# Pooled q and k in four buffers, v of batch 0 pooled by additions, mask cast on GpSimd, and a new order from the planner

## The chip, the cores and the metric

The kernel runs on one core of a Trainium2 chip. The core has a matrix engine (TensorE, PE in the profile; PEld is its weight load), three engines for elementwise work (VectorE, DVE; ScalarE, ACT; GpSimd, POOL) and a queue engine (SyncE, SP) that issues most of the transfers from device memory. Each engine works through a list of its own in order; they meet at semaphores. The metric is the time of one execution on the device in microseconds.

## What is computed

Attention over 4 batches of 8 heads with 576 positions of 64 channels, in two parts that are added: one on q, k and v averaged over groups of four positions (144 each), whose result is repeated four times, and one in a band of 7 keys around each position. Its output, 2304 rows of 512 channels, goes through two feed-forward blocks. All in float32.

```python
q_d, k_d, v_d = (x.reshape(B, H, S // 4, 4, D).mean(axis=3) for x in (q, k, v))
out_up = np.repeat(sm_attn(q_d, k_d, v_d), 4, axis=2)
mask = np.abs(pos[:, None] - pos[None, :]) < 4
out_local = softmax(where(mask, scale * q @ k.T, -1e9)) @ v
x = (out_up + out_local).transpose(0, 2, 1, 3).reshape(2304, 512)
...
h = x @ w_in                     # 512 -> 2048
x = (s * np.maximum(h, 0) ** 2 + b) @ w_out
...
out = ((x @ w_a) * (x @ w_b)) @ w_out2   # 512 -> 1536 -> 512
```

## The kernel before

The matmuls of the feed-forward blocks run at full TensorE speed on numbers split in a high and a low part (`xsh`, `xsl`; `gh`, `gl`), with three products for each. The weights come as 64-bit words; a slice of 512 KB (`w_a`, `w_o`) is turned into its two parts on ScalarE and VectorE in steps (ScalarE's L349, L342 and L378, VectorE's L354, L362 and L383). The first block has 32 slices. It works on six blocks of 384 positions with 16 steps each: a step has 12 products `h` (L1059 to L1061), then ScalarE's relu (L1076), square (L1080) and cast (L1083), then VectorE's rest `gl` (L1087), then 12 products `acc` (L1102 to L1104). The second block (`ab`, L1347) comes behind.

Attention has to deliver a block's x before its first `h`. Two stages do it. In the ramp stand the first eight band tiles of 96 positions, the pooled part of batches 0 and 1, and all 32 weight slices. In the band stage, which opens only behind the last task of the ramp, because it takes over its memory, the remaining positions are worked on VectorE (L908, L914, L969), along with the pooled parts of batches 2 and 3.

The pooled part goes by pairs of heads, four for a batch. For a pair: load k and q, sum groups of four into `kd`, `qd` (VectorE L582 for batch 0, GpSimd L584 and L585 for batch 1), scores `sc` on TensorE (L620), maximum `nb` (L634), its scaling (L637), exponentials on ScalarE (L647), a normalizing product (L662), transposes `at` (L671), copies (L683), then the product with pooled v, `o` (L691), copied to `up` (L703). For batch 0 the pooled v, `vp`, is a reduction on VectorE (L603). For the other batches `pv` is summed by transfers: SyncE issues a plain one (L549) for each half of the keys, and GpSimd issues three that accumulate onto each (L551), six in all. A band tile has scores (L774, L780), exponentials (L816), transposes (L839) and `o` (L857).

What stands where in each engine's list is decided by a planner in the kernel's own Python. Every piece of work is a task with an engine, an estimated duration, what it reads, the buffers and tokens that it takes and gives back, and a due time. `Program.order` always takes the task that can start earliest, and of equal ones the one due first; it also puts filler products `pw` on `wz` between TensorE's ramp tasks. Instructions are emitted in that order. Buffer counts (`RAMP_BUFS`) and tokens limit how far a list can run ahead: loaded slices have four tokens, `MAX_STAGED`. Durations and due times are constants in the source, so a change of them changes the order of the lists and nothing else.

Of the kernel before, what the change touches and what calls it, by code (L numbers as in the profile page):

```python
# [23 lines left out]
TQ = 96  # L24
# [31 lines left out]
MAX_STAGED = 4  # L56

# [3 lines left out]
T0, STEP = 40.2, 4.018 / 384  # L61
LEAD = 26.6
DUE_DOWN = (12.1, 7.8, 2.1, 22.5)
DUE_NEXT = (60.0, 0.0)
DUE_TILE = (8.3, 20.6, 22.0)
DUE_JOB = (11.6, 11.7, 14.9)

WARM, FILL_MIN, FILL_MAX = 18, 1, 20

RAMP_BUFS = {"dq": 2, "dk": 2, "dv": 2, "qd": 1, "kd": 1, "vp": 4, "tq": 1, "tk": 1, "tv": 2, "e": 1, "x": 1, "z": 2}  # L70
# [39 lines left out]
class Program:  # L110
# [26 lines left out]
    def order(self):  # L137
# [9 lines left out]
        clock, warming = Clock(), True  # L147
# [10 lines left out]
        while len(out) < len(self.tasks):  # L158
            best = None
            for e in ENGINES:  # L160
                for t in avail[e]:
                    s = max(at[e], t.ready)
                    picks, fs = [], []
# [42 lines left out]
            at[t.eng] = t.end  # L206
            avail[t.eng].remove(t)
# [26 lines left out]
def moe_chain(ctx, tc, qT, kT, vd, tq, tk, tv, qu, ku, vu, w_a1, w_o1, w_a2, w_b2, w_o2, sb, ident_d, bmask_d, emask_d, out):  # L234
# [19 lines left out]
    ones = const.tile([128, 2], F32, name="ones")  # L254
    bc = const.tile([128, HP], F32, name="bc")
# [19 lines left out]
    def load(dst_src, nbytes, reads=(), writes=(), acq=(), rel=(), due=1e9, after=()):  # L275
# [18 lines left out]
    def i_fn(picks):  # L294
        nc.sync.dma_start(out=ident, in_=ident_d)
        V.tensor_copy(out=identb, in_=ident[:TQ, :TQ])

    def m_fn(picks):
        bm = new("r", "tq", [128, HP, TQ])[:TQ].rearrange("p a b -> p (a b)")[:, :3 * TW].rearrange("p (a b) -> p a b", a=3)
        nc.sync.dma_start(out=bm, in_=bmask_d)  # L300
        V.tensor_copy(out=bmaskb, in_=bm)
# [3 lines left out]
    def consts():  # L305
        add("SP", 0.5, i_fn, writes=["ident"])
        add("SP", 0.5, m_fn, writes=["const"], acq=[("rtq",)], rel=["rtq"])
# [99 lines left out]
    def w_out(p, t, after, due=1e9):  # L407
# [8 lines left out]
        if t == 0:  # L416
# [12 lines left out]
            wait = [add("SP", 1.5, s_fn, [("wz", t, p)], [("wod", p)])]  # L429
# [109 lines left out]
    def pool_in(b, after, due):  # L539
# [18 lines left out]
    def down(b, hp, ph, pool_eng, v_eng, due=1e9):  # L558
# [16 lines left out]
        for name, src in (("k", "dk"), ("q", "dq")):  # L575
            eng = pool_eng[name == "q"]

            def prep(p, name=name, eng=eng):
# [9 lines left out]
                eng, dve(S) if eng == "DVE" else 1.25, prep, [(src, key)], [(name + "d", key)],  # L588
                [(ph + name + "d",)], [ph + (dq if src == "dq" else src)] if b else (),
            )  # L590
        if b == 0:
            for kh in range(2):
                def lv(p, kh=kh):
                    st["v", kh] = new(ph, "dv", [HK, 4, 2 * D])
                    return st["v", kh], vd[b, hp, :, kh]

                load(lv, HK * 2048, writes=[("dv", key, kh)], acq=[(ph + "dv",)], after=after)

                def vprep(p, kh=kh):
                    x = st["v", kh]  # L600
                    d = st["vp", kh] = new(ph, "vp", [HK, 2 * D])
                    if v_eng == "DVE":
                        V.tensor_reduce(out=d, in_=x.rearrange("p r c -> p c r"), axis=AX.X, op=ALU.add)  # L603
                    else:
                        G.tensor_tensor(out=x[:, 0:2], in0=x[:, 0:2], in1=x[:, 2:4], op=ALU.add)
                        G.tensor_tensor(out=d, in0=x[:, 0], in1=x[:, 1], op=ALU.add)

                add(
                    v_eng, dve(512) if v_eng == "DVE" else 1.1, vprep, [("dv", key, kh)], [("vp", key, kh)],
                    [(ph + "vp",)], [ph + "dv"],  # L610
                )

        def vpool(kh):
            return st["vp", kh] if b == 0 else pooled[b][:, kh, hp]

        def s_fn(p):
# [9 lines left out]
            "PE", 1.0, s_fn, [("qd", key), ("kd", key)], [("sc", key)], [wide, wide, E_SLOT[ph]],  # L626
# [49 lines left out]
        tt = add("PE", 0.55, t_fn, [("a", key), "ident"], [("at", key)], [wide, wide], lead=LEAD, share=0.5625)  # L676
# [10 lines left out]
        def o_fn(p):  # L687
# [9 lines left out]
            "PE", 0.6, o_fn, [("aT", key), ("upslot", b)] + ([("vp", key, 0), ("vp", key, 1)] if b == 0 else [("pv", b)]),  # L697
            [("o", key)], [wide], [pick(ts, 2)] + ([ph + "vp", ph + "vp"] if b == 0 else ["pv"] if hp == HP - 1 else []),
# [845 lines left out]
    for hp in range(HP):  # L1544
        down(0, hp, "r", DOWN_ENG[hp], "DVE", target(0) - DUE_DOWN[0] + DUE_DOWN[1] * hp)
# [145 lines left out]
```

## Time and profile before

| | |
|---|---|
| median of 3 runs | 935.74 us (934.76 to 935.96) |
| span of the profiled execution, first to last instruction | 932.3 us |
| TensorE busy | 913.2 us, 98% |
| VectorE busy | 789.9 us, 85% |
| ScalarE busy | 497.4 us, 53% |
| GpSimd busy | 69.7 us, 7% |
| moved by transfers | 96.76 MB, 104 GB/s in the mean |

The profile is of one execution; its page gives the span, not the whole time of that execution, which holds 3.4 us more if it was like the median. Busy shares are means over stages that differ: a row of a window tells more than the page's first line. Busy time of TensorE includes the filler products.

### The profile page before, as it was taken

How to read it: one execution, taken by the hardware profiler on the slowest of the kernel's cores; microseconds unless marked ns; L12 is line 12 of the kernel's file. 1: busy time of each engine (PE TensorE's matmuls, PEld its weight loads, DVE VectorE, ACT ScalarE, POOL GpSimd, SP SyncE). 2: the span in 40 equal slices, each digit the busy share in tenths (PEclk: the TensorE clock that was granted, in tenths of full speed). 3: DMA queues.
4: the chain of work that ended last, by engine and by line, in shares of the span. 5: the costliest groups of instructions: out<-in, count | busy, mean ns of one | idle time of the engine just before them, and what ended most of it. 6: DMA issues, size and time to landing. Idle time of an engine off the chain costs nothing.

```text
span 932.3 us, 14367 instructions
## 1 busy us (share of the span) xinstructions
PE 913.2 (98%) x5319; PEld 847.0 (91%) x5319; DVE 789.9 (85%) x1388; ACT 497.4 (53%) x1144; POOL 69.7 (7%) x70
## 2 busy tenths in 40 slices
PE   8988999999999999999999999999999999999997
PEld 4667989998999899999999999999999999999996
DVE  6988998999999999995977999879877778877753
ACT  4989995345445443535988555335433336433322
POOL 2241201021322200000000000000000000000000
PEclk9998999999999999999999999999999999999999
DMA  7869626224354332313477342012200010300001
GB/s 206 241 174 332 156 90 194 82 82 133 115 115 114 103 107 69 102 29 136 148 262 261 122 122 82 23 44 81 102 22 3 24 43 13 102 29 18 1 1 69
DMA packets 46864, 96.76 MB, mean 104 GB/s; under 512 B 6393, under 2 KB 21337, under 8 KB 46409
## 3 DMA queue, kind: packets, MB, share of 16 engines
q1 hardware_dynamic: 39160, 92.77, 31.0%
q0 software_dynamic: 7200, 2.67, 2.5%
q8 instruction: 42, 0.69, 0.3%
q10 hardware_dynamic: 432, 0.39, 0.1%
q14 instruction: 30, 0.24, 0.1%
HBM read 83.22 MB, written 12.58 MB: 103 GB/s over the span
## 4 chain that ended last, share of the span: by engine, by line
PE 84%; DVE 5%; ACT 4%; issue 3%; DMA 2%; POOL 1%; SPq 0%; ACTq 0%
PE ab L1347 28%; PE acc L1102 7%; PE acc L1103 6%; PE h L1059 6%; PE acc L1104 6%; PE h L1061 6%; PE h L1060 6%; PE acc L1488 5%; PE acc L1489 5%; PE acc L1487 5%; DVE pr L969 1%; DMA pv<-in_vd_dram 1%; ACT z L342 1%; DMA tq<-in_bmask_dram 1%; ACT w L378 1%
## 5 line engine op out<-in xcount | busy, mean ns | idle before, releaser
L1347 PE MATMUL ab<-xo,w 128*128 128x384 f32 x1376 | 273.7, 338 | 0.4 <-DVE u L1390 0.4
L1347 PEld LDWEIGHTS ab<-xo,w 128*128 128x128 f32 x1376 | 246.1, 188 | 16.3 <-DVE u L1390 0.7
L1102 PE MATMUL acc<-gh,w 128*128 128x384 f32 (+1 forms) x384 | 134.2, 350 | 4.0 <-ACT w L816 2.0
L1103 PE MATMUL acc<-gl,w 128*128 128x384 f32 x384 | 131.2, 342 | 0.0
L1059 PE MATMUL h<-xsh,w 128*128 128x384 f32 x384 | 131.1, 341 | 0.0
L1104 PE MATMUL acc<-gh,w 128*128 128x384 f32 (+1 forms) x384 | 130.5, 340 | 0.0
L1061 PE MATMUL h<-xsh,w 128*128 128x384 f32 x384 | 129.0, 336 | 0.0
L1060 PE MATMUL h<-xsl,w 128*128 128x384 f32 x384 | 129.0, 336 | 0.0
L1076 ACT ACTIVATE u<-h 128x384 f32<-128x384 f32 x96 | 47.1, 491 | 116.3 <-PE h L1061 114.9
L1463 ACT ACTIVATE gh<-u 128x384 fp32r<-128x384 f32 x69 | 36.2, 524 | 84.6 <-DVE u L1424 50.5
L1102 PEld LDWEIGHTS acc<-gh,w 128*128 128x128 f32 x384 | 73.0, 190 | 8.1 <-ACT w L816 2.6
L1059 PEld LDWEIGHTS h<-xsh,w 128*128 128x128 f32 x384 | 72.2, 188 | 2.4 <-issue 2.0
L1103 PEld LDWEIGHTS acc<-gl,w 128*128 128x128 f32 x384 | 73.1, 190 | 0.9 <-DVE gl L1087 0.9
L1104 PEld LDWEIGHTS acc<-gh,w 128*128 128x128 f32 x384 | 73.0, 190 | 0.0
L1060 PEld LDWEIGHTS h<-xsl,w 128*128 128x128 f32 x384 | 72.2, 188 | 0.0
L1061 PEld LDWEIGHTS h<-xsh,w 128*128 128x128 f32 x384 | 72.1, 188 | 0.0
L1087 DVE TENSOR_TENSOR gl<-u,gh 128x384 fp32r<-128x384 f32 x96 | 54.3, 565 | 15.4 <-ACT gh L1083 15.2
L1371 ACT ACTIVATE w<-ab 128x384 f32<-128x384 f32 x31 | 15.2, 491 | 95.2 <-PE ab L1347 93.4
L1489 PE MATMUL acc<-w,gl 128*128 128x512 f32 x138 | 54.4, 394 | 0.0
L1488 PE MATMUL acc<-w,gh 128*128 128x512 f32 x138 | 54.3, 394 | 0.0
L1487 PE MATMUL acc<-w,gh 128*128 128x512 f32 x138 | 54.2, 393 | 0.0
L354 DVE TENSOR_SCALAR w<-w 128x512 uint16<-128x512 f32 x61 | 45.6, 767 | 8.3 <-ACT w L349 8.0
(207 smaller groups left out, 1743.9 us busy)
## 6 DMA issues: line engine op xcount, KB each, us to landing
w<-in_w_a_dram SPq DMA_DIRECT2D x26, 512.0 KB
w<-in_w_o_dram SPq DMA_DIRECT2D x25, 512.0 KB
bk<-in_ku_dram SPq DMA_DIRECT2D x22, 320.0 KB
bk<-in_vu_dram SPq DMA_DIRECT2D x22, 320.0 KB
w<-wod SPq DMA_DIRECT2D x12, 512.0 KB
w<-in_w_b_dram SPq DMA_DIRECT2D x10, 512.0 KB
x2d<-ev SPq DMA_DIRECT2D x24, 192.0 KB
x<-x2d SPq DMA_DIRECT2D x3, 1536.0 KB
```

What stands on the lines that cost most here:

```text
L1059: nc.tensor.matmul(out=st["h"], lhsT=w[:, 0, k], rhs=hi[:, k], start=(k == 0), stop=False)
L1060: nc.tensor.matmul(out=st["h"], lhsT=w[:, 0, k], rhs=lo[:, k], start=False, stop=False)
L1061: nc.tensor.matmul(out=st["h"], lhsT=w[:, 1, k], rhs=hi[:, k], start=False, stop=(k == HP - 1))
L1076: A_.activation(out=st["u"], in_=st["h"], func=ACTF.Relu)
L1087: V.tensor_tensor(out=st["lo"], in0=st["u"], in1=st["hi"][:, :n].bitcast(F32), op=ALU.subtract)
L1102: nc.tensor.matmul(out=acc, lhsT=wh, rhs=st["hi"], start=(f == 0), stop=False)
L1103: nc.tensor.matmul(out=acc[:, :n], lhsT=wh, rhs=st["lo"], start=False, stop=False)
L1104: nc.tensor.matmul(out=acc, lhsT=wl, rhs=st["hi"], start=False, stop=(f == FA - 1))
L1347: nc.tensor.matmul(out=o, lhsT=w[:, k], rhs=x, start=(not more and k + n == 0), stop=(k == 1 and n == 2), skip_group_check=more,)
L1487: nc.tensor.matmul(out=acc, lhsT=gh, rhs=w[:, 0], start=first, stop=False)
L1488: nc.tensor.matmul(out=acc, lhsT=gh, rhs=w[:, 1], start=False, stop=False)
L1489: nc.tensor.matmul(out=acc, lhsT=gl, rhs=w[:, 0], start=False, stop=last)
```

## The change

Six edits, and a new order of all lists that follows from them and from new constants.

1. `qd` and `kd` of the ramp get four buffers each instead of one.
2. v of batch 0 is loaded by one transfer of 288 KB for each pair (before, two of 144 KB into buffers of their own), into a slot of the weight pool, and pooled in place by two VectorE additions over 512 and 256 elements; before, by two reductions.
3. The first thing on ScalarE is an exponential of two numbers, so that the function table is loaded there.
4. The casts of the mask and of the identity stand on GpSimd.
5. The planner models a transfer by its 16 engines: how many of them it takes, the time on each, a queue of eight for SyncE, and 0.46 us for the issue. Before, a load held SyncE for its bytes at 235 GB/s, and an accumulating transfer held GpSimd for 1.25 us and was seen 6 us later.
6. Due times, lead and some durations are new; `FILL_MIN` falls from 1 to 0.

```diff
-T0, STEP = 40.2, 4.018 / 384
+T0, STEP = 26.9, 4.018 / 384
...
-RAMP_BUFS = {"dq": 2, "dk": 2, "dv": 2, "qd": 1, "kd": 1, "vp": 4, "tq": 1, "tk": 1, "tv": 2, "e": 1, "x": 1, "z": 2}
+RAMP_BUFS = {"dq": 2, "dk": 2, "qd": 4, "kd": 4, "tq": 1, "tk": 1, "tv": 2, "e": 1, "x": 1, "z": 2}
...
+ISSUE, QUEUE, DMA_START, POOL_START, DMA_LAND = 0.46, 8, 1.0, 1.4, 0.95
...
+                    if e == "SP" and len(landed) >= QUEUE:
+                        s = max(s, landed[-QUEUE])
...
+            for n, (engines, took) in enumerate(t.dma):
+                first = s + (DMA_START + ISSUE * n if t.eng == "SP" else POOL_START)
+                for j in range(engines):
+                    wire[j] = max(wire[j], first) + took
+                done = max(wire[:engines]) + DMA_LAND
+                t.end = max(t.end, done)
+                if t.eng == "SP":
+                    landed.append(done)
...
+def wires(rows, pieces, size, each=0.0):
+
+    n = max(i for i in range(1, 17) if rows % i == 0)
+    return n, rows // n * pieces * (each or 0.010 + size / 25e3)
...
-        return add("SP", max(0.45, nbytes / 235e3), fn, reads, writes, acq, rel, due, after)
+        dma = [wires(rows, pieces, nbytes / rows / pieces)]
+        return add("SP", ISSUE, fn, reads, writes, acq, rel, due, after, seen=0.1, dma=dma)
...
         V.memset(ones, 1.0)
+        A_.activation(out=warm, in_=ones, func=ACTF.Exp)
...
-        V.tensor_copy(out=bmaskb, in_=bm)
+        const_eng.tensor_copy(out=bmaskb, in_=bm_of["bm"])
...
                 t[kh] = add(
-                    "POOL" if r else "SP", 1.25, fn, (), [("pv", b)] if r == 3 else (), () if r + kh else [("pv",)], (), due,
-                    [t[kh]] if r else [t[0]] if kh else after, seen=6.0,
+                    "POOL" if r else "SP", 1.25 if r else ISSUE, fn, (), [("pv", b)] if r == 3 else (), () if r + kh else [("pv",)], (), due,
+                    [t[kh]] if r else [t[0]] if kh else after, seen=0.1, dma=[wires(HK, HP, 512, 0.065 if r else 0)],
                 )
...
-                    if v_eng == "DVE":
-                        V.tensor_reduce(out=d, in_=x.rearrange("p r c -> p c r"), axis=AX.X, op=ALU.add)
...
+            def vprep(p):
+                x = st["v"]
+                V.tensor_tensor(out=x[:, :, 0:2], in0=x[:, :, 0:2], in1=x[:, :, 2:4], op=ALU.add)
+                V.tensor_tensor(out=x[:, :, 0], in0=x[:, :, 0], in1=x[:, :, 1], op=ALU.add)
```

How the lists change at the places that matter. GpSimd's list begins, before, with the first accumulating transfer, pools one head pair of batch 1 (`dk`, `dq` are the loaded tiles), and has four more transfers next:

```order
6 L551 DMA pv<-in_vd_dram 72x4x128
7 L584 ISA
8 L584 TENSOR_TENSOR dk<-dk 128x144x2
9 L585 TENSOR_TENSOR kd<-dk 128x144
10 L584 TENSOR_TENSOR dq<-dq 128x144x2
11 L585 TENSOR_TENSOR qd<-dq 128x144
12 L551 DMA pv<-in_vd_dram 72x4x128 x4
13 L584 TENSOR_TENSOR dk<-dk 128x144x2
```

Of the change, from the end of the second pair on, with two casts and the poolings of two pairs ahead of these rows:

```order
16 L621 TENSOR_TENSOR qd<-dq 128x144
17 L587 DMA pv<-in_vd_dram 72x4x128
18 L620 TENSOR_TENSOR dk<-dk 128x144x2
19 L621 TENSOR_TENSOR kd<-dk 128x144
20 L620 TENSOR_TENSOR dq<-dq 128x144x2
21 L621 TENSOR_TENSOR qd<-dq 128x144
22 L620 TENSOR_TENSOR dk<-dk 128x144x2
23 L621 TENSOR_TENSOR kd<-dk 128x144
24 L587 DMA pv<-in_vd_dram 72x4x128
25 L620 TENSOR_TENSOR dq<-dq 128x144x2
26 L621 TENSOR_TENSOR qd<-dq 128x144
27 L587 DMA pv<-in_vd_dram 72x4x128 x10
```

The poolings moved ahead of the transfers: of batch 1's six, one comes behind two pairs, one behind nearly four, and four behind all of them (the other six of the last row are batch 2's). In SyncE's list the plain transfer of `pv` moved from the 11th place to the 26th.

TensorE's list at the first products `h`, before (`sc`, `at` and `o` on `w`, `e` are batch 1's pooled part):

```order
236 L1059 MATMUL h<-xsh,w 128x384
237 L1060 MATMUL h<-xsl,w 128x384
238 L1061 MATMUL h<-xsh,w 128x384
239 L620 MATMUL sc<-kd,qd 72x144 x4
240 L671 MATMUL at<-ident,w 72x72 x8
241 L691 MATMUL o<-w,pv 64x144 x4
242 L774 LDWEIGHTS identb
243 L774 MATMUL sc<-bmaskb,identb 96x408
```

And of the change, from the last of the first twelve `h` to the first `acc`:

```order
289 L1089 MATMUL h<-xsh,w 128x384
290 L699 MATMUL at<-ident,w 72x72 x8
291 L719 MATMUL o<-e,pv 64x144 x4
...
297 L699 MATMUL at<-ident,w 72x72 x8
298 L719 MATMUL o<-w,pv 64x144 x4
299 L699 MATMUL at<-ident,w 72x72 x8
300 L719 MATMUL o<-w,pv 64x144 x4
301 L867 MATMUL at<-ident,w 102x96 x8
302 L719 MATMUL o<-w,pv 64x144 x4
303 L1130 MATMUL acc<-gh,w 128x386
```

All four scores of batch 1 moved ahead of the first `h`, and all four products with `pv` stand between the first twelve `h` and the first `acc`; before, the first six `h` stood ahead of the last score, and more `h` between the products with `pv`.

## Rows read from the trace of the kernel before

**Rows 1.** The page, busy us of each engine over the span.

```profile
PE 913.2 (98%) x5319; PEld 847.0 (91%) x5319; DVE 789.9 (85%) x1388; ACT 497.4 (53%) x1144; POOL 69.7 (7%) x70
```

**Rows 2.** Busy time by stretches, from the span's start; granted clock, transfers at the end.

```profile
core 0: us, PE busy (x) PEld busy (x) DVE busy (x) ACT busy (x) POOL busy (x), PEclk, DMA share, GB/s
0.00:10.00 10.00, 8.86 (x42) 4.19 (x44) 3.56 (x8) 0.00 (x0) 0.20 (x4) 1.00 0.82 267
0.00:72.50 72.50, 63.48 (x581) 41.45 (x581) 60.16 (x137) 53.46 (x224) 21.38 (x26) 0.98 0.74 205
73.00:144.00 71.00, 67.34 (x392) 63.60 (x389) 63.74 (x122) 68.06 (x159) 8.85 (x6) 0.95 0.61 183
150.00:200.00 50.00, 50.00 (x289) 49.71 (x289) 48.70 (x60) 22.04 (x44) 3.87 (x5) 1.00 0.41 120
```

**Rows 3.** Timeline of ScalarE: start, us, instruction; idle time before it and its releaser.

```profile
11.24 1.28 ACT L647 ACT_TABLE_LOAD   x1 [11.24 <-DVE nb L637]
...
57.97 0.84 ACT L683 ACTIVATE w<-at 72x288 f32<-72x288 f32 x2 [3.17 <-PE at L671]
...
143.89 0.49 ACT L1076 ACTIVATE u<-h 128x384 f32<-128x384 f32 x1 [1.62 <-PE h L1061]
```

**Rows 4.** Timeline of TensorE, 54 to 72 us.

```profile
54.69 1.24 PE L620 MATMUL sc<-kd,qd 64*72 64x144 f32 x8 [2.55 <-POOL qd L585]
...
61.76 0.71 PE L691 MATMUL o<-w,pv 72*64 72x144 f32 x8
...
63.73 0.70 PE L671 MATMUL at<-ident,w 72*72 72x72 f32 x8
64.36 0.71 PE L691 MATMUL o<-w,pv 72*64 72x144 f32 x8
```

**Rows 5.** Timeline of VectorE, 145 to 147 us.

```profile
145.53 0.56 DVE L1087 TENSOR_TENSOR gl<-u,gh 128x384 fp32r<-128x384 f32 x1 [2.53 <-ACT gh L1083]
...
146.44 2.02 DVE L908 TENSOR_TENSOR pr<-bq,bk 128x1792 f32<-128x1792 f32 x1 [0.28 <-DMA bq<-in_qu_dram]
```

**Rows 6.** Chain of work that ended last, 0 to 110 us: start, us, what.

```profile
4.66 5.86 DMA tq<-in_bmask_dram
```

**Rows 7.** VectorE by lines, 0 to 73 us: busy us, mean ns, idle before.

```profile
L603 DVE TENSOR_REDUCE vp<-dv 72x128 f32<-72x512 f32 x8 | 8.2, 1032 | 0.1
...
L662 DVE TENSOR_TENSOR w<-w,sm 72x576 f32<-72x576 f32 x6 | 4.7, 780 | 0.0
...
L301 DVE CAST bmaskb<-tq 96x306 bf16<-96x306 f32 x1 | 0.3, 320 | 0.3 <-DMA tq<-in_bmask_dram 0.3
```

**Rows 8.** Timeline of GpSimd, 10 to 60 us: the accumulating transfers of batch 1.

```profile
12.01 1.32 POOL L551 DMA_DIRECT2D pv<-in_vd_dram  x1 [11.57 <-DMA pv<-in_vd_dram]
...
19.54 1.22 POOL L551 DMA_DIRECT2D pv<-in_vd_dram  x1
26.05 1.19 POOL L551 DMA_DIRECT2D pv<-in_vd_dram  x1 [5.29 <-issue]
31.79 1.20 POOL L551 DMA_DIRECT2D pv<-in_vd_dram  x1 [4.55 <-issue]
42.14 1.19 POOL L551 DMA_DIRECT2D pv<-in_vd_dram  x1 [9.15 <-issue]
...
49.15 1.22 POOL L551 DMA_DIRECT2D pv<-in_vd_dram  x1 [1.89 <-DMA pv<-in_vd_dram]
```

**Rows 9.** ScalarE by lines, 0 to 73 us.

```profile
L816 ACT ACTIVATE e<-sc,tnb 96x102 f32<-96x102 f32 x8 | 2.6, 340 | 0.6 <-DVE tnb L805 0.6
```

**Rows 10.** Waits, 10 to 73 us: total us, times, longest us.

```profile
ACT w L647 <- DVE nb L637: 2.6, 3, 1.8
```

**Rows 11.** Transfers, 10 to 56 us, then 95 to 117: KB each, median us to landing.

```profile
DMA packets 6663, 9.23 MB, mean 201 GB/s; under 512 B 1229, under 2 KB 3715, under 8 KB 6657
...
pv<-in_vd_dram POOLq DMA_DIRECT2D x6, 144.0 KB, 6.4
...
pv<-in_vd_dram POOLq DMA_DIRECT2D x4, 144.0 KB, 4.7
```

More of the change, by code (lines that the diff above doesn't have):

```diff
@@ L146, in order @@
         at = {e: 0.0 for e in ENGINES}
-        clock, warming = Clock(), True
+        clock, warming, wire = Clock(), True, [0.0] * 16
+        landed = []
+        at["SP"] = 0.75
         at["PE"] = clock.run(1.07, 0.17 * WARM, 1.0)
@@ L273, in keep_warm, with load @@
             nc.tensor.matmul(out=pw[0], lhsT=wz[:, :128], rhs=wz, start=True, stop=True)
-    def load(dst_src, nbytes, reads=(), writes=(), acq=(), rel=(), due=1e9, after=()):
+    def load(dst_src, nbytes, reads=(), writes=(), acq=(), rel=(), due=1e9, after=(), rows=128, pieces=1):
         def fn(picks):
@@ L292, in warm_fn, with ic_fn, bm_src, mc_fn @@
         V.memset(ones, 1.0)
[L294 to L300, printed above, removed]
-        V.tensor_copy(out=bmaskb, in_=bm)
+        A_.activation(out=warm, in_=ones, func=ACTF.Exp)
+    const_eng = ENG[CONST_ENG][1]
+    def ic_fn(picks):
+        eng = const_eng
+        eng.tensor_copy(out=identb, in_=ident[:TQ, :TQ])
+    bm_of = {}
+    def bm_src(picks, h=0):
+        if h == 0:
+            bm = new("r", "tq", [128, HP, TQ])[:TQ].rearrange("p a b -> p (a b)")[:, :3 * TW].rearrange("p (a b) -> p a b", a=3)
+            bm_of["bm"] = bm
+        return bm_of["bm"], bmask_d
+    def mc_fn(picks):
+        const_eng.tensor_copy(out=bmaskb, in_=bm_of["bm"])
     add("CTL", 0.0, warm_fn, acq=[("acc",)], due=-1e6)
     def consts():
-        add("SP", 0.5, i_fn, writes=["ident"])
-        add("SP", 0.5, m_fn, writes=["const"], acq=[("rtq",)], rel=["rtq"])
+        load(lambda p: (ident, ident_d), 128 * 512, writes=["ident"], due=DUE_CONST)
+        load(bm_src, TQ * 3 * TW * 4, writes=["bm"], acq=[("rtq",)], due=DUE_CONST, rows=TQ)
+        name, _, cost = ENG[CONST_ENG]
+        add(name, cost(128), ic_fn, ["ident"], ["const"], due=DUE_CONST + 5)
+        add(name, cost(3 * TW), mc_fn, ["bm"], ["const"], rel=["rtq"], due=DUE_CONST + 5)
     a_src = [(w, f) for f in range(FA) for w in (w_a1, w_o1)]
@@ L591, in down, with lv @@
         if b == 0:
[L592 to L601, printed above, removed]
-                    if v_eng == "DVE":
-                        V.tensor_reduce(out=d, in_=x.rearrange("p r c -> p c r"), axis=AX.X, op=ALU.add)
[L604 to L611, printed above, removed]
+            def lv(p):
+                st["v"] = slot(p[0], F32).rearrange("p a m -> p (a m)").rearrange("p (k r d) -> p k r d", k=2, r=4)[:HK]
+                return st["v"], vd[b, hp]
+            tv0 = load(lv, HK * 4096, writes=[("dvl", key)], acq=[("w",)], after=after, rows=HK)
+            def vprep(p):
+                x = st["v"]
+                V.tensor_tensor(out=x[:, :, 0:2], in0=x[:, :, 0:2], in1=x[:, :, 2:4], op=ALU.add)
+                V.tensor_tensor(out=x[:, :, 0], in0=x[:, :, 0], in1=x[:, :, 1], op=ALU.add)
+            add("DVE", dve(512) + dve(256), vprep, [("dvl", key)], [("dv", key)])
         def vpool(kh):
-            return st["vp", kh] if b == 0 else pooled[b][:, kh, hp]
+            return st["v"][:, kh, 0] if b == 0 else pooled[b][:, kh, hp]
         def s_fn(p):
@@ L767, in qk @@
             return w[:, t0:t0 + TQ] if name == "q" else w[:, t0 - 3 + k0:t0 - 3 + k1]
-        load(l_v, TW * DM * 4, writes=[("tv", i)], acq=[(names["tv"],)], after=after)
+        load(l_v, TW * DM * 4, writes=[("tv", i)], acq=[(names["tv"],)], after=after, rows=TW)
         def s_fn(p):
```

54 lines of the change are left out of this document (31 added, 23 removed).

## The prediction, made before the changed kernel ran

> **What bounds the kernel now.** Begin with the page and the table by stretches. TensorE is busy for 98% of the span [rows 1], and from 150 us on it has no gap: 50.00 of 50 us [rows 2]. That part is matmuls in a fixed order, and the change adds or removes none of them. So whatever the change gives or costs must be settled before about 145 us, in the ramp, and then it shifts everything behind it.
>
> In the ramp TensorE is not the limit, although it reads as busy: many of its rows are the filler products on `wz`. ScalarE is. It does nothing until 11.24 us, where it first waits for VectorE's scaled maximum and then loads its table, 1.28 us [rows 3]. After that it is busy for 53.46 us of the first 72.5 and for 68.06 of the 71 us from 73 to 144 [rows 2]. Its largest later wait is 3.17 us at 57.97 for a transpose of TensorE [rows 3], and that transpose stands behind scores of batch 1 for which TensorE waited 2.55 us on GpSimd's pooled q [rows 4]. ScalarE's list of the ramp has all 32 weight slices in it, and the bands may open only when the last ramp task is done: VectorE's first band product starts at 146.44 [rows 5]. From there VectorE is the other full engine, 48.70 of 50 us [rows 2]. An end of the ramp that is G earlier or later therefore moves the end by about G, as TensorE's stream and VectorE's band move together.
>
> **The change, part by part, along ScalarE.**
>
> Start. The fourth q tile is issued ahead of the mask, and the mask has landed by 4.66 + 5.86 = 10.52 [rows 6]. With four buffers VectorE no longer waits for the first scores before it pools pairs 2 to 4, so at the latest at 10.5 + 0.75 it has pooled all four and scales the first maximum. Its list now has that scale behind the fourth pair, so the first exponential starts at about 11.3. Before, it started behind the table load, 11.24 + 1.28 = 12.52. Gain 1.2 us. The moved table load is hidden while ScalarE idles for 11 us; uncovered it would cost its 1.28 us.
>
> VectorE. Eight reductions of v, 8.2 us together, become four pairs of additions over 512 and 256 elements. The nearest row is the addition-like product over 576 elements, 780 ns [rows 7]: 0.69 + 0.35 us per pair, 4.2 us in all. The mask's cast (0.32) and that of the identity go to GpSimd. VectorE has some 4.4 us less to do by 60 us. That is no term by itself, since ScalarE sets the end; it only shortens ScalarE's waits for VectorE. GpSimd's casts have no row; between VectorE's 0.32 us [rows 7] and the 1.2 us of a transfer that GpSimd issues [rows 8], they fit into the time before the first band scores, and GpSimd idles there.
>
> ScalarE's list. I counted its rows in both lists up to the last copy of a pooled transpose of batch 1, the row behind which it waits for `up` of batch 1. The new list has there the same exponentials of the pooled parts, 16 copies and 6, 5 and 5 steps of the weight slices that the old one has reached at 72.5 us; it has eight more exponentials of a band tile, 2.6 us [rows 9], and four `up` copies and two steps of the first product fewer, about 1.5. So that place is worth 53.46 - 1.28 + 1.1 = 53.3 us of ScalarE's work, and the old kernel is as far at 72.5 + 1.1 = 73.6. The new one, if nothing held it but 2.5 us of short waits (my estimate: the old one idles 72.5 - 11.24 - 53.46 = 7.8 us on this way; 3.2 of them are the wait at 57.97 and 2.6 the three waits for maxima [rows 10], which the four pooled pairs take away; the 2.0 left, and a little more), would be there at 11.3 + 53.3 + 2.5 = 67.1, a gain of 6.5 us.
>
> **The wait that the change adds: the pooled v of batch 1.** GpSimd now pools q, k of two head pairs first, and its six accumulating transfers `pv` come behind. Look at the six starts of the old kernel: 12.01, 19.54, 26.05, 31.79, 42.14, 49.15 [rows 8]. Three of the pauses between them are put down to issue: the next one starts only when the one before has landed. Five steps take 37.14 us, 7.43 each, 5.74 to 10.35, and in a quieter stretch the median to landing is 4.7 us instead of 6.4 [rows 11]. This chain can't be compressed by order. Its start moves back: the plain transfer that the first one adds to is now 26th in SyncE's list. Ahead of it and with it go 7.45 MB (eight tiles of 288 KB, mask and identity 179 KB, v 1152, tv 408, four q, k 1152, tq and tk 396, three slices of 512, itself 144 KB). At the 267 GB/s of the first 10 us [rows 2] that is 27.9 us; at the mean of 201 GB/s [rows 11] it is 37. The first figure is nearer, since the queue is never empty there. The poolings ahead of it on GpSimd need tiles that are loaded before it.
>
> So: first step at 27.9, beside the slices, keys and queries issued at once (2.4 MB), taken at the longest row, 10.35 [rows 8]; five more at the middle of the two medians, 5.55. The last lands at 27.9 + 10.35 + 27.75 = 66.0. TensorE has, behind the first twelve products `h` and one transpose, `o<-e,pv` as the next row; nothing passes it. From that row to the copy of the last transpose the old trace shows the same sequence: 61.76 `o`, scores, 63.73 transposes, 64.36 `o`, then transposes and a copy, about 5 us [rows 4]. The new ScalarE thus reaches the compared place at 66.0 + 5.0 = 71.0 instead of 73.6. **Gain 2.6 us**, 3.9 of the free 6.5 lost to the wait. TensorE, idle for some us there, may drop to the low level of its clock, as the granted clock shows before for part of the ramp (0.95 in the mean from 73 to 144 [rows 2]); an extra 1 to 2 us is inside the range.
>
> Behind that place the two lists do the same work: 27 slices less one step, one band tile, fifteen `h` chains. ScalarE had only 2.9 us of idle time there, so I carry the 2.6 on unchanged to the opening of the bands. The new due times within the bands reorder work that fills both engines; I take nothing for them, plus or minus 1.5. In time: 932.3 of span [rows 1] and the 3.4 that lie between it and the median of 935.74; 935.7 - 2.6 = **933.1 us**.
>
> **A rule that speaks for more.** The old trace has six accumulating transfers at 4.7 to 10.4 us each. The Trainium skill, "DMA: Bandwidth & Descriptors", section on the anatomy of a software-generated DMA, gives about 2.0 us plus the bytes over 436 GB/s. For 147 KB that is an estimate of 2.3 us, so that the chain would end at 28 + 14 = 42 and hide; the trace does not agree with it here.
>
> **The rivals.**
>
> *Pooled v in time.* If the chain lands by 62 it is covered: 67.1 less the 5 us behind it. That needs 34 us for six steps, 5.7 each, which one of the old five reaches (5.74) and two come near (6.51, 7.01), and the new kernel has more of its loads done before 35 us. Then the gain is the free one, 935.7 - 6.5 = **929.2**. The rule just named falls under this case. Chance 0.25.
>
> *Pooled v much later: slower.* If the six steps keep the old 7.43, the chain ends at 27.9 + 44.6 = 72.5, ScalarE is at the place at 77.5, 3.9 later than the old one: **939.6**. It decides from a landing at 68.6 us on. For it speaks that the old mean was taken at a similar load; against it, that the slices are limited by four staging tokens, so after 35 us fewer transfers compete. Chance 0.20.
>
> *No change.* VectorE's band starts behind the last product chain of block 0, where VectorE waited 2.53 us for ScalarE and that 1.62 us for TensorE [rows 3, 5]. If TensorE's own backlog (in the new order 12 products `h` stand ahead of the last pooled output of batch 1, in the old one 24) ends the ramp there, the gain is used up: **935.7**. Chance 0.13.
>
> *Forecast*, the wait shortens the gain: 0.42, from 931 to 935.
>
> **The numbers.** About 0.2%, 1.9 us, is what a measurement of this kernel can tell from none. Of the forecast's 0.42, 0.29 is faster by that, 0.10 within it, 0.03 slower. Faster: 0.29 + 0.25 = 0.54. Within: 0.10 + 0.13 + 0.01 of the late case = 0.24. Slower: 0.03 + 0.19 = 0.22. The range goes from 2 us under the early case to the late one less 1: 927.0 to 938.6; it leaves out a tenth on either side.
>
> **What would show it.** Right: the first exponential near 11.3; the first `pv` on GpSimd between 25 and 31 us and the last landing between 61 and 71; TensorE idle, for 2 us or more, ahead of `o<-e,pv`, released by a transfer; the first band product at 143 to 145. Wrong: no idle time ahead of that row (then the early case), ScalarE idling for longer before it (then the 2.5 us of short waits were mis-sized), or a gap of TensorE behind 150 us, for which I have no term.

## The result and the profile after

| | before | after |
|---|---|---|
| median, measured together | 935.85 us (934.76 to 937.30) | 948.96 us (947.67 to 949.82) |
| ratio | 1 | 1.0144 (1.0125 to 1.0163) |
| span of the profiled execution | 932.3 us | 946.9 us |
| mean granted clock | 0.994 | 0.987 |

The changed kernel is 13 us slower; 933.1 us, with a range up to 938.6, was forecast. In the ratios of the runs below, one execution of e5_both (973.8 us at a mean granted clock of 0.867) and one of the kernel before (2019.2 us) were in a slower state and are left out. The page after, which answers to [rows 1]: TensorE has some 8 us more busy time, for the same matmuls and a few more fillers.

```profile
PE 921.5 (97%) x5341; PEld 851.4 (90%) x5341; DVE 785.5 (83%) x1386; ACT 496.9 (52%) x1145; POOL 74.3 (8%) x72
```

Three landmarks cut the span of the profiled execution, each a place in TensorE's list: the 97th product `h` (step 8 of the first block), the 961st (step 80), and the 85th product `ab` of the second block.

| | ramp: start to `h` 97 | bands: to `h` 961 | transition: to `ab` 85 | rest |
|---|---|---|---|---|
| before | 108.3 | 330.1 | 86.4 | 407.5 |
| after | 115.7 | 329.5 | 95.1 | 406.6 |
| difference | +7.4 | -0.6 | +8.7 | -0.9 |

So there are two losses, far apart, and between the last two landmarks TensorE has the same 489 products in both kernels. First the ramp. The busy time by stretches after, as in [rows 2]: from 60 to 80 us TensorE works 11.75 of 20 us, ScalarE 9.54, VectorE 8.54, and the granted clock, as a share of TensorE's full clock, is 0.63; in the next stretch it is 0.86. The last row belongs to the transition.

```profile
core 0: us, PE busy (x) PEld busy (x) DVE busy (x) ACT busy (x) POOL busy (x), PEclk, DMA share, GB/s
60.00:80.00 20.00, 11.75 (x83) 8.62 (x81) 8.54 (x21) 9.54 (x36) 2.38 (x2) 0.63 0.30 73
80.00:100.00 20.00, 20.00 (x130) 18.46 (x129) 13.30 (x26) 16.93 (x47) 2.38 (x2) 0.86 0.89 313
525.00:550.00 25.00, 22.18 (x108) 20.39 (x109) 20.50 (x39) 10.14 (x18) 0.00 (x0) 0.93 0.14 46
```

The same two stretches of the ramp before; only the first differs much, as the clock of 0.86 stands here too:

```profile
60.00:80.00 20.00, 17.42 (x146) 13.34 (x144) 18.35 (x41) 19.98 (x63) 1.21 (x1) 0.97 0.85 269
80.00:100.00 20.00, 19.98 (x118) 19.45 (x119) 17.06 (x32) 18.87 (x50) 2.85 (x2) 0.86 0.98 323
```

TensorE's timeline there (start, us, instruction, idle time before it and its releaser), which answers to [rows 4]: two waits for the pooled v, 8.25 us together, and behind them rows that take nearly twice their time, 1.17 for eight transposes against 0.66 ahead of the waits and 0.70 in [rows 4].

```profile
61.36 0.66 PE L699 MATMUL at<-ident,w 72*72 72x72 f32 x8
66.80 0.75 PE L719 MATMUL o<-e,pv 72*64 72x144 f32 x4 [4.77 <-DMA pv<-in_vd_dram]
71.02 0.75 PE L719 MATMUL o<-e,pv 72*64 72x144 f32 x4 [3.48 <-DMA pv<-in_vd_dram]
...
74.15 1.17 PE L699 MATMUL at<-ident,w 72*72 72x72 f32 x8
...
81.29 0.69 PE L1130 MATMUL acc<-gh,w 128*128 128x386 f32 x1
```

The chain of waits from 0 to 90 us (start, length, what) says why the pooled v is late: a key tile lands 12.35 us after its issue, and the plain transfer issued then needs 8.54.

```profile
11.43 12.35 DMA dk<-in_kT_dram
23.80 8.54 DMA pv<-in_vd_dram
...
67.06 3.91 DMA pv<-in_vd_dram
```

GpSimd's six accumulating transfers, which answer to [rows 8], run from 32.65 to 67.06 + 3.91 = 70.97 us.

```profile
32.65 1.79 POOL L587 DMA_DIRECT2D pv<-in_vd_dram  x1 [2.55 <-DMA pv<-in_vd_dram]
...
43.30 1.22 POOL L587 DMA_DIRECT2D pv<-in_vd_dram  x1 [3.83 <-issue]
...
48.06 1.21 POOL L587 DMA_DIRECT2D pv<-in_vd_dram  x1 [2.31 <-issue]
54.21 1.20 POOL L587 DMA_DIRECT2D pv<-in_vd_dram  x1 [4.94 <-issue]
59.98 1.19 POOL L587 DMA_DIRECT2D pv<-in_vd_dram  x1 [4.58 <-issue]
67.06 1.20 POOL L587 DMA_DIRECT2D pv<-in_vd_dram  x1 [5.89 <-issue]
```

ScalarE (timeline, as [rows 3]) has its first exponential at 11.62 instead of 12.53, idles 8.93 us for a transpose, and is at the compared place, the end of the last copy of a pooled transpose of batch 1, at 77.14 + 0.89 = 78.0 us.

```profile
11.62 0.38 ACT L675 ACTIVATE e<-sc,nb 72x144 f32<-72x144 f32 x1 [9.39 <-DVE nb L665]
...
74.88 0.89 ACT L711 ACTIVATE w<-at 72x288 f32<-72x288 f32 x2 [8.93 <-PE at L699]
77.14 0.89 ACT L711 ACTIVATE w<-at 72x288 f32<-72x288 f32 x2 [1.38 <-PE at L699]
```

VectorE's first band product starts 6.24 us later than in [rows 5]:

```profile
152.68 2.02 DVE L936 TENSOR_TENSOR pr<-bq,bk 128x1792 f32<-128x1792 f32 x1 [0.37 <-DMA bq<-in_qu_dram]
```

The second loss is where the first block hands over to the second. The waits of TensorE (total us, times, longest) from 470 to 550 us; the last row is the kernel before's, which has only this one there:

```profile
PE ab L1376 <- DVE w L1440: 2.8, 1, 2.8
PE acc L1131 <- DVE gl L1115: 0.7, 3, 0.3
PE acc L1130 <- ACT gh L1111: 0.7, 2, 0.4
...
PE ab L1347 <- DVE u L1390: 0.4, 1, 0.4
```

They add up to 4.2 us of the 8.7 lost. Behind the longest of them the granted clock falls again, to 0.93 in the mean of 525 to 550 us, which is worth about 1.8 us (an estimate: 0.07 of 25 us); the kernel before has 1.00 there. Where the remaining 2.5 to 3 us went is not shown. These waits are the ends of a longer story, which the chain of waits from 470 to 545 us tells: weight slices of the second block, each landing over 5 us after its issue, with ScalarE's conversion (L385) behind it.

```profile
474.04 5.42 DMA w<-in_w_o_dram
...
485.30 5.16 DMA wx<-in_w_a_dram
...
492.94 5.43 DMA wx<-in_w_o_dram
...
504.53 7.78 DMA w<-in_w_a_dram
...
520.68 1.13 ACT ev L1157 x2
521.83 0.32 SPq L1175
522.24 5.27 DMA w<-in_w_o_dram
527.59 0.69 ACT w L385
...
531.15 0.47 DVE w L1440
531.67 8.09 PE ab L1376 x36
```

Read the last link backwards. TensorE waits for an addition on VectorE, which stands in VectorE's list behind steps of a slice, which wait for ScalarE, which waits for a slice (`w_o`) that this addition does not even use. SyncE issued it at 522.24, behind two stores (L1175) that waited for ScalarE's `ev`. All three lists are followed in order, so one late load holds them all.

### The profile page after: what moved, and what is told of

Same layout as the page of the kernel before. It is cut to its first block, busy times and chain, and to the rows that moved or that the text cites. A ratio compares the mean times of both kernels' runs of the same rounds, so it can differ in the third digit from the quotient of the medians.

```text
span 946.9 us, 14405 instructions
## 1 busy us (share of the span) xinstructions
PE 921.5 (97%) x5341; PEld 851.4 (90%) x5341; DVE 785.5 (83%) x1386; ACT 496.9 (52%) x1145; POOL 74.3 (8%) x72
## 4 chain that ended last, share of the span: by engine, by line
PE 77%; DMA 8%; ACT 5%; DVE 4%; issue 4%; POOL 1%; SPq 1%; ACTq 0%; POOLq 0%; DVEq 0%
PE ab L1376 28%; PE acc L1130 5%; PE acc L1517 5%; PE acc L1518 5%; PE acc L1516 5%; PE acc L1131 5%; PE h L1087 5%; PE acc L1132 5%; PE h L1088 5%; PE h L1089 5%; DMA wx<-in_w_a_dram 1%; DMA pv<-in_vd_dram 1%; DMA dk<-in_kT_dram 1%; DMA w<-in_w_o_dram 1%; PE o L719 1%
## 5 line engine op out<-in xcount | busy, mean ns | idle before, releaser
L1376 PE MATMUL ab<-xo,w 128*128 128x384 f32 x1376 | 282.5, 340 | 2.9 <-DVE w L1440 2.8
L1492 ACT ACTIVATE gh<-u 128x384 fp32r<-128x384 f32 x68 | 35.6, 524 | 89.9 <-DVE u L1453 48.2
L1111 ACT ACTIVATE gh<-u 128x384 fp32r<-128x384 f32 x96 | 50.4, 525 | 3.1 <-PE acc L1132 1.3
L1108 ACT ACTIVATE u<-u 128x384 f32<-128x384 f32 x96 | 50.4, 526 | 1.8
L1518 PE MATMUL acc<-w,gl 128*128 128x512 f32 x129 | 50.8, 394 | 0.0
L1517 PE MATMUL acc<-w,gh 128*128 128x512 f32 x129 | 50.8, 394 | 0.0
```

The lines of the kernel that those rows point to most:

```text
L1108: A_.activation(out=st["u"], in_=st["u"], func=ACTF.Square)
L1111: A_.activation(out=st["hi"][:, :n], in_=st["u"], func=ACTF.Copy)
L1376: nc.tensor.matmul(out=o, lhsT=w[:, k], rhs=x, start=(not more and k + n == 0), stop=(k == 1 and n == 2), skip_group_check=more,)
L1517: nc.tensor.matmul(out=acc, lhsT=gh, rhs=w[:, 1], start=False, stop=False)
L1518: nc.tensor.matmul(out=acc, lhsT=gl, rhs=w[:, 0], start=False, stop=last)
```

## The experiments

The table has all runs, with times in us, the ratio to the kernel before on the same chip, and the landmarks of the profiled execution. These are of one execution each; those of e8_pv_cost and e13_tv_first2 are the slowest of their kernels, that of e7_land the fastest.

| run | median | ratio (95%) | `h` 97 at | transition |
|---|---|---|---|---|
| e1_pv_early | 940.77 | 1.0070 (1.0037 to 1.0103) | 105.7 | 95.8 |
| e6_fill | 943.95 | 1.0078 (1.0057 to 1.0099) | 108.4 | 97.5 |
| e8_pv_cost | 944.79 | 1.0101 (1.0040 to 1.0163) | 117.8 | 96.0 |
| e2_second_old | 938.58 | 1.0010 (0.9992 to 1.0027) | 112.5 | 87.1 |
| e7_land | 942.29 | 1.0065 (1.0043 to 1.0086) | 111.2 | 89.0 |
| e5_both | 931.89 | 0.9972 (0.9925 to 1.0019) | 105.9 | 87.1 |
| e15_both_again | 931.35 | 0.9970 (0.9943 to 0.9997) | 106.2 | 87.1 |
| e3_edits_old_plan | 931.30 | 0.9948 (0.9925 to 0.9970) | 110.0 | 86.4 |
| e14_edits_again | 931.76 | 0.9958 (0.9938 to 0.9979) | 108.0 | 86.4 |
| e4_new_plan_old_edits | 954.81 | 1.0190 (1.0165 to 1.0215) | 123.1 | 95.7 |
| e9_table | 934.94 | 0.9993 (0.9974 to 1.0012) | 109.2 | 86.4 |
| e10_bufs | 936.50 | 1.0017 (1.0002 to 1.0032) | 110.1 | 86.2 |
| e12_adds | 941.04 | 1.0064 (1.0039 to 1.0090) | 118.7 | 86.3 |
| e11_tv_first | 935.33 | 0.9999 (0.9982 to 1.0016) | 109.4 | 86.4 |
| e13_tv_first2 | 936.14 | 1.0012 (0.9984 to 1.0039) | 121.0 | 86.4 |

**The ramp: is it the pooled v?** The list that the planner returns is changed in eight places before it is emitted.

```diff
+        move(("v", 1, 0, 0), tag["tv", 1])
+        move(("v", 1, 0, 1), tag["v", 1, 0, 0])
+        move(("v", 1, 1, 0), tag["cast"])
+        for n, (r, kh) in enumerate(((1, 1), (2, 0), (2, 1), (3, 0))):
+            move(("v", 1, r, kh), tag["q", 1, n])
+        move(("v", 1, 3, 1), tag["v", 1, 3, 0])
```

> The changed kernel with one thing moved: the eight transfers that pool v of batch 1. Its two plain transfers stand right behind the second tv load in SP's list (about 11 us, before: 23.8 and 32.4 us), and the six accumulating ones are spread between the pairs of kd and qd in GpSimd's list. The orders of TensorE, VectorE and ScalarE stay as they are. Theory A (pooled v late, and half clock behind it, is the first of two losses): its last transfer lands near 55 us instead of 71, `o<-e,pv` waits under 1 us, the first acc product starts near 72 to 74 us instead of 81.3, and the kernel takes 941 to 944 us instead of 949; the second loss, some 9 us of TensorE's waits between 475 and 550 us, stays. Rival B (what holds the ramp is SP's list, which issues nothing between 58.7 and 81.4 us, or ScalarE's own order): the first acc product comes at 79 us or later, and the time is 947 to 950 us.

GpSimd's first accumulating transfer (timeline) comes at 22.39 and the last at 54.54:

```profile
22.39 1.33 POOL L588 DMA_DIRECT2D pv<-in_vd_dram  x1 [10.27 <-DMA pv<-in_vd_dram]
...
54.54 1.20 POOL L588 DMA_DIRECT2D pv<-in_vd_dram  x1 [3.71 <-issue]
```

TensorE's timeline shows no idle time ahead of `o<-e,pv`, full speed, and the first `acc` 8.2 us sooner:

```profile
66.36 0.71 PE L720 MATMUL o<-e,pv 72*64 72x144 f32 x8
...
73.10 0.45 PE L1131 MATMUL acc<-gh,w 128*128 128x386 f32 x1
```

The ramp's landmark moves from 115.7 to 105.7, 2.6 us ahead of the kernel before, and the transition keeps its loss. Theory A holds, although the last transfer lands only at 58.9 us (55 expected) and the time is a little under its range; B, that another list holds the ramp, falls.

**Wait or clock?** The pooled v stays late, but TensorE multiplies zeros while it waits.

```diff
             for kh in range(2):
+                for _ in range((70, 50)[kh] if (b, hp) == (1, 0) else 0):
+                    nc.tensor.matmul(
+                        out=o, lhsT=wz[:, :128], rhs=wz[:, :SD], start=(kh == 0), stop=(kh == 0), skip_group_check=True
+                    )
                 for h in range(2):
```

> The changed kernel, its pooled v as late as it is, but with 70 small products of zeros ahead of the first `o<-e,pv` and 50 more between its two halves (they add zeros, the result is unchanged), so that TensorE works while it waits. Theory A (of the ramp's loss, the wait is one half and the lower clock behind it the other): the wait stays, `o<-e,pv` still ends at about 71.5 us, the granted clock of 60 to 80 us rises from 0.63 to above 0.9, the stretch from there to the first acc product shrinks from 10.3 us to 6 or 7, and the time is 944 to 946 us. Rival B (that stretch is set by ScalarE and VectorE, not by the clock): 948 to 950 us.

TensorE's timeline and the stretch that had a clock of 0.63:

```profile
62.01 4.54 PE L719 MATMUL o<-wz 128*128 128x144 bf16 x70
66.48 0.47 PE L723 MATMUL o<-e,pv 72*64 72x144 f32 x4
66.87 3.30 PE L719 MATMUL o<-wz 128*128 128x144 bf16 x50
70.10 0.47 PE L723 MATMUL o<-e,pv 72*64 72x144 f32 x4
...
75.83 0.45 PE L1134 MATMUL acc<-gh,w 128*128 128x386 f32 x1
```

```profile
60.00:80.00 20.00, 20.00 (x246) 17.61 (x245) 11.63 (x26) 13.17 (x46) 1.85 (x2) 1.00 0.41 108
```

From the second half of that `o` to the first `acc` it takes 75.83 - 70.10 = 5.7 us, against 81.29 - 71.02 = 10.3 in the changed kernel: 4.5 us were the clock. The ramp then ends at 108.4, as in the kernel before.

One execution could be chance, but e2_second_old and e7_land, further down, have every list of the ramp in the same order, without the zeros. The second half of `o` in their timelines:

```profile
68.32 0.75 PE L722 MATMUL o<-e,pv 72*64 72x144 f32 x4 [5.81 <-DMA pv<-in_vd_dram]
...
67.28 0.75 PE L720 MATMUL o<-e,pv 72*64 72x144 f32 x4 [5.54 <-DMA pv<-in_vd_dram]
```

| | second half of `o` | from there to the first `acc` | from there to `h` 97 |
|---|---|---|---|
| after | 71.02 | 10.3 | 44.6 |
| e2_second_old | 68.32 | 10.3 | 44.1 |
| e7_land | 67.28 | 10.3 | 43.9 |
| e6_fill | 70.10 | 5.7 | 38.3 |

So with the same order v lands anywhere from 67 to 71 us, and behind it the clock costs 5.5 to 6.3 us by the ramp's end. Of the ramp's 10.0 us between the changed kernel and e1_pv_early, 6.3 are the clock and 3.7 the wait itself. (In e6_fill v landed at 69.0, and the zeros held TensorE for 1.1 us more.)

**Does the planner place v late because it holds its transfers for short?**

```diff
-                    "POOL" if r else "SP", 1.25 if r else ISSUE, fn, (), [("pv", b)] if r == 3 else (), () if r + kh else [("pv",)], (), due,
-                    [t[kh]] if r else [t[0]] if kh else after, seen=0.1, dma=[wires(HK, HP, 512, 0.065 if r else 0)],
+                    "POOL" if r else "SP", 1.25, fn, (), [("pv", b)] if r == 3 else (), () if r + kh else [("pv",)], (), due,
+                    [t[kh]] if r else [t[0]] if kh else after, seen=6.0,
```

> The changed kernel with one cost changed: the pooling transfers of v are planned as in the kernel before (1.25 us each and 6.0 us until they are seen) in place of the transfer model. The planner then puts their first plain load ahead of the tv loads by itself, and the rest of the order follows from the plan. Theory A (this cost is what put them late): no wait of `o<-e,pv` above 1 us, the first loss gone, the second there as before, 939 to 944 us. Rival B (the new due times put the ramp's work in an order that loses elsewhere): 947 us or more.

The first accumulating transfer did come at 18.38 us, but everything else was reordered too: the last one is issued at 60.41, and in the profiled execution the wait was there (waits of TensorE, 0 to 150 us):

```profile
PE o L719 <- DMA pv<-in_vd_dram: 6.0, 1, 6.0
```

Four executions took 940.2 to 953.6 us, the two short ones at a mean granted clock of 0.996 and 0.997, the long ones at 0.986 and 0.988. Theory A asked for no wait, and fails as put: the cost alone moves the first transfer, but a new plan has its own waits. What in the new numbers puts v late is not settled.

**The transition: is it the order of loads?** From the second block's first task on, the costs of the kernel before are used.

```diff
+        if old:
+            return add("SP", max(0.45, nbytes / 235e3), fn, reads, writes, acq, rel, due, after)
         dma = [wires(rows, pieces, nbytes / rows / pieces)]
...
+    old.append(1)
     x_open([opened])
```

> The changed kernel, with only the tasks of the second block (loads of its weights, stores, its products) planned at the costs of the kernel before; the ramp and the bands keep their order word for word. Theory A (the transition's order of loads, from the plan's new transfer model, is the second loss): TensorE's waits between 475 and 550 us fall from 9 us to about 1, and the kernel takes 939 to 942 us. Rival B (the transition only pays for something that came late from the ramp): no more than 2 us are won, 946 to 950 us.

The transition falls from 95.1 to 87.1 us, and the stretches from 475 to 550 us have nearly no idle time of TensorE, as their table shows. Theory A holds, though the 9 us of waits that it names are the lost time; the waits themselves were 4.2 and are 0.7 here. The time gained, 10 us, is 2 more than the transition's 8.0; the ramp of the same order took 112.5 us in this execution and 115.7 in the changed kernel's.

```profile
475.00:500.00 25.00, 25.00 (x145) 25.00 (x144) 17.01 (x26) 19.79 (x38) 0.00 (x0) 1.00 0.76 265
500.00:525.00 25.00, 24.34 (x138) 23.54 (x137) 18.88 (x33) 18.68 (x36) 0.00 (x0) 1.00 0.65 240
525.00:550.00 25.00, 25.00 (x132) 23.23 (x131) 25.00 (x49) 12.93 (x24) 0.00 (x0) 1.00 0.27 87
```

**Which part of the cost?** One number: when a load of the second block counts as landed.

```diff
-        return add("SP", ISSUE, fn, reads, writes, acq, rel, due, after, seen=0.1, dma=dma)
+        return add("SP", ISSUE, fn, reads, writes, acq, rel, due, after, seen=2.05 if old else 0.1, dma=dma)
```

> The changed kernel with one number changed, for the second block's loads alone: the plan sees each of them land 1.95 us later, so 5.3 us after its issue for a weight slice, as the chain of the changed kernel's trace shows (5.16 to 5.43 us), in place of 3.34 us. All else of the new planner stays. Theory A (the transition is lost because the plan holds these loads for landed 2 us too soon): TensorE's waits between 475 and 550 us fall from 9 us to 3 or less, 940 to 943 us. Rival B (it is that a load no longer holds SP for its bytes in the plan, so that loads stand in another order): they stay above 6 us, 946 to 950 us.

The transition takes 89.0 us, 6.1 of the 8.7 lost. What stays are two waits (470 to 550 us):

```profile
PE ab L1377 <- DVE w L1441: 1.8, 1, 1.8
PE ab L1377 <- DVE w L1407: 0.8, 1, 0.8
```

So most of this loss is that the plan believes a slice of 512 KB there 2 us before it is. Of the remaining 2.6 us, e2_second_old has 1.9 back with the rest of the old costs (which of them is open), and 0.7 stay even there.

**Both steps together**, the two diffs above in one kernel.

> Both earlier steps in one kernel: the pooling transfers of batch 1 moved ahead (as in e1_pv_early) and the second block planned at the old costs (as in e2_second_old). Theory A (two separate losses, at 62 to 82 us and at 475 to 550 us): the gains add, 949 less 8 less 10, so 929 to 932 us, below the kernel before. Rival B (one loss that shows in two places, so that either step repays most of it): 936 to 939 us.

> e5_both once more, beside the others on one chip, since its five runs lay between 930.2 and 941.2 us with one disturbed. Theory A (the changed kernel with both losses mended is faster than the kernel before): 930 to 934 us, a ratio below 0.998. Rival B (no measurable difference): 934.5 to 938 us.

931.9 us in the first run, whose interval still holds 1, and 931.35 in the second, whose interval ends just below it: the losses add, and with both mended the changed kernel is about 0.3% faster than the kernel before.

**Edits or order?** The code edits with the planner and numbers of before, and the reverse. Two places of the first, against the changed kernel:

```diff
-T0, STEP = 26.9, 4.018 / 384
+T0, STEP = 40.2, 4.018 / 384
...
-        return add("SP", ISSUE, fn, reads, writes, acq, rel, due, after, seen=0.1, dma=dma)
+        return add("SP", max(0.45, nbytes / 235e3), fn, reads, writes, acq, rel, due, after)
```

> The edits of code alone (pooled q and k in four buffers, v of batch 0 by two additions from one load, table load first, casts on GpSimd), ordered by the kernel before's planner, costs and due times. Theory A (the edits are harmless or help; the order costs): 930 to 937 us. Rival B (an edit itself costs, such as the larger load of v of batch 0 or the cast on GpSimd): 940 us or more.

> The reverse: the code edits of the kernel before (one buffer each for pooled q and k, v of batch 0 by reductions in halves, no early table load, casts on VectorE), ordered by the new planner with its transfer model, costs and due times. Theory A (the order costs): 944 to 955 us, with a wait of `o<-e,pv` or of the second block's weights to be seen. Rival B (only edits and order together cost): 938 us or less.

> e3_edits_old_plan once more, beside the others on one chip. Theory A (the edits in the old order win 4 to 5 us): 930 to 933 us, a ratio below 0.998. Rival B (931.3 us belonged to that chip or hour; since no edit by itself won anything, the edits together do not either): 934.5 to 936.5 us, as e11_tv_first, which differs from it by four places in SP's list.

The edits alone win 0.5 and 0.4% in two measurements, so that gain is no chance; the new order alone, without them, costs 1.9%. Each planner makes its own order of the edits that it is given, so "order" here is a planner with its numbers. In that sense the change comes apart: its edits help by 4 to 6 us, its order costs 18 to 19 (949.0 against 931.3 with the edits, 954.8 against 936.2 without). The loss is not at the same place each time: in e4_new_plan_old_edits the transition takes 95.7 us, but TensorE's longest wait in the ramp is 5.7 us for VectorE's `qd`, not for the pooled v.

What goes along with the edits' gain is the clock. The ten executions of e3_edits_old_plan have mean granted clocks of 0.993 to 0.999, the 25 of the kernel before beside them 0.985 to 0.998; the one of these at 0.998 took 929.8 us, and the two with the edits at 0.998 took 929.0 and 929.3. What keeps the clock up in that order is not shown.

**Which edit wins?** Three of the four, each alone in the kernel before; the casts on GpSimd were not tried alone. The early table load:

```diff
+    warm = const.tile([128, 2], F32, name="warm")
...
         V.memset(ones, 1.0)
+        A_.activation(out=warm, in_=ones, func=ACTF.Exp)
```

> The kernel before with the early table load alone (one small exponential ahead of all else on ScalarE); all orders stay word for word. Theory A (the load is hidden, and the first exponential comes 1.2 us sooner, but a later wait absorbs it): first exponential at 11.2 to 11.4 us instead of 12.53, time within 0.2% of 936. Rival B (the start is on the path to the end): 1.2 us less in the median, 934.7 us, and every later milestone of TensorE 1.2 us sooner.

The first exponential starts at 11.15 us, 1.4 sooner than in [rows 3], and the time is the same within 0.2%. The interval of the time would also hold the 1.2 us of rival B, but the landmark `h` 97, at 109.2 against 108.3, does not come sooner: a later wait takes the gain, as in theory A.

```diff
-RAMP_BUFS = {"dq": 2, "dk": 2, "dv": 2, "qd": 1, "kd": 1, "vp": 4, "tq": 1, "tk": 1, "tv": 2, "e": 1, "x": 1, "z": 2}
+RAMP_BUFS = {"dq": 2, "dk": 2, "dv": 2, "qd": 4, "kd": 4, "vp": 4, "tq": 1, "tk": 1, "tv": 2, "e": 1, "x": 1, "z": 2}
```

> The kernel before with four buffers each for pooled q and k in the ramp, in place of one, and the kernel before's planner and numbers. Theory A (the one buffer was what TensorE waited for at 54.69 us, 2.5 us for a pooled q, and what the plan spread the score products over): the wait goes, 932 to 934.5 us. Rival B (the buffers alone win nothing, the next wait comes at once): 935 to 938 us.

No gain, as in rival B. TensorE's wait for GpSimd's `qd` is gone, others (2.4 us for ScalarE, 1.9 for a tv load) are new.

```diff
...
-                        V.tensor_reduce(out=d, in_=x.rearrange("p r c -> p c r"), axis=AX.X, op=ALU.add)
...
+                V.tensor_tensor(out=x[:, :, 0:2], in0=x[:, :, 0:2], in1=x[:, :, 2:4], op=ALU.add)
+                V.tensor_tensor(out=x[:, :, 0], in0=x[:, :, 0], in1=x[:, :, 1], op=ALU.add)
```

> The kernel before with one edit: v of batch 0 by one load for each pair of heads and two additions, in place of two loads and two reductions. Planner and numbers as before. Theory A (VectorE has slack here, so that its 4.4 us less work win nothing by themselves): within 2 us of the kernel before. Rival B (VectorE, or the eight loads in place of four, were on the ramp's path): 930 to 933 us.

Slower by 5.6 us, which neither theory had: the old planner, given this edit, orders the ramp so that TensorE waits 4.3 us for GpSimd's `qd` and 3.7 for VectorE's `w`, and the ramp ends at 118.7. None of the three wins alone; all four together, in the order that the old planner makes of them, do. Why that order is better is not settled.

**A small load behind large ones.** In e3_edits_old_plan TensorE waits 6.0 us for a tv load that SyncE issues behind four weight slices. The slices are moved behind that load; then two of them behind the next one as well.

```diff
+        move(("w", 1), tag["tv", 3])
+        for k in (2, 3, 4):
+            move(("w", k), tag["w", k - 1])
```

> As e3_edits_old_plan (the code edits in the old plan's order, 931.3 us), with one tv load moved ahead of four weight slices in SP's list: there TensorE waited 6.0 us for it at 46.6 us, and its granted clock fell to 0.83 in 40 to 60 us. Theory A (that wait and the clock behind it are on the path): the wait goes, the clock of 40 to 60 us is 1.00, and 2 to 5 us are won, 926 to 930 us. Rival B (ScalarE and VectorE, not TensorE, are behind at that place, or the weights now come too late): 931 us or more.

> As e11_tv_first, with two of the four weight slices moved behind the next tv load as well (in e11_tv_first the wait of 6 us only went from one tv load to the next, which stood behind the four slices). Theory A (the small load waits for the bytes of the slices ahead of it): that tv load lands some 4 us sooner, `o<-e,tv` waits under 3 us instead of 5.9, and 1 to 3 us are won against the same kernel without the moves. Rival B (what bounds the ramp there is ScalarE and VectorE): no difference to it.

In e11_tv_first that tv load lands in 4.28 us, and the next, now behind the slices, in 8.82 (chain of waits); TensorE's wait only went there, 5.88 us:

```profile
41.97 4.28 DMA tv<-in_tv_dram
...
46.31 8.82 DMA tv<-in_tv_dram
```

In e13_tv_first2 it is 0.86 there and 3.65 at the one behind. The small load does wait for the slices, but mending it place by place moves the wait down the list. Both expectations of a gain are misses, and more than that: at ratios of 0.9999 and 1.0012, against 0.9948 and 0.9958 without the moves, the 4 us that the edits had won are gone. Why so much is lost with the wait only moved is not shown.

## Why the prediction was wrong, step by step

**Right.** The first exponential, 11.62 (11.3 forecast). VectorE's work, 4.4 us less (789.9 to 785.5). The new wait, its place and its kind: TensorE idle ahead of `o<-e,pv`, released by a transfer. The six steps, 38.1 us forecast, 70.97 - 32.65 = 38.3 measured, each 3.9 to 10.4 from issue to landing. The Trainium skill, "DMA: Bandwidth & Descriptors", section on the anatomy of a software-generated DMA, gave an estimate of 2.3 us for each of the six; the trace after, with its 3.9 to 10.4, does not agree with it either. The bands: nothing taken, within 1.5, and -0.6 measured.

**Mis-sized: the first step's start.** "27.9", from 7.45 MB at the rate of the first 10 us. The plain transfer was issued at 23.80 and took 8.54, so the first step came at 32.65: the same bytes at 230 GB/s, between the two rates that the prediction had. That is 4.75 of the 5.0 us by which v was late. Its landing at 70.97 is beyond the 68.6 us from which the rival "pooled v much later" decides; in e2_second_old and e7_land, with the same lists in the ramp, the first step comes at 31.2 and v lands at 68.3 and 67.2, short of that bound, so how late v is differs from one execution to the next.

**Mis-sized: "about 5 us"** from the pooled v to the compared place. It took 7.0, so that place was reached 4.4 us later than before (78.0 against 73.6), and more was lost behind it, up to the band product's +6.2, because TensorE ran at the low clock after its idle time. The prediction allowed 1 to 2 us for that; the four executions above show 5.5 to 6.3 at the ramp's end. So the ramp went the way of that rival, at a higher price than its 3.9.

**Mis-sized: the free path.** The gain that the rival "pooled v in time" held for free, 6.5, is 2.6 at the landmark in e1_pv_early. There v is in time, and ScalarE, busy for all of 60 to 80 us, is at the compared place at 71.6, not at 67.1.

**Failed: "whatever the change gives or costs must be settled before about 145 us".** That TensorE had no gap behind 150 us, taken from a row of 150 to 200 us, was read as a property of the work. It was one of the order of loads: the transition's matmuls are the same, but their operands pass through SyncE's, ScalarE's and VectorE's lists, and the new transfer model reorders those too. The prediction named this case as one "for which I have no term", and gave it neither a chance nor a price. It cost 8.7 us, the larger loss; e2_second_old alone takes 8.0 of it away, and e7_land shows that most of it, 6.1, is a landing time put 2 us too early.

## What to carry to other kernels

A planner's transfer model is a change to every stage that it orders: look in each at what the new model believes a load takes, and lay it beside the issue and landing of such a load in the trace, before trusting that a stage without gaps stays without. A transfer that TensorE waits for can have two prices, the wait and the clock behind it. Here the second was the larger, and products that do nothing bought it back. An order's edit and a code's edit should be timed apart: here the order cost some 18 us and the edits gave 4 to 6.

## What had not been expected of the hardware

TensorE at work on zeros, 7.8 us of them, kept the granted clock at 1.00; idle for 8.25 us, it came back at 0.63 in the mean of 60 to 80 us and 0.86 in the next 20, which is the lower of its two levels (1.2 and 2.4 GHz) for a part of each. Executions of one kernel can differ by several us along with the clock: twelve of e13_tv_first2 took 933.4 to 944.9 us, the longest at a whole-run mean clock of 0.983 and, from 60 to 80 us, of 0.50, with TensorE busy for 19.24 of these 20 us; ten of e15_both_again took 929.6 to 932.4 at 0.993 to 0.996, and two 938.8 and 940.7 at 0.987 and 0.988.
